# Keys of four attention layers kept in HBM by chunk and loaded 128 overlapping rows at a time

## Chip, cores and metric

One core of one Trainium2 chip. The metric is the device time of one execution in microseconds. A ratio is the mean time of one kernel's fast runs over that of the other's of the same rounds, so it is not quite the ratio of the medians quoted beside it.

## The reference

Four residual attention layers over 2048 positions of width 640, with 32 heads of 20 features. Layers 0 and 2 see a window of 256 keys, layers 1 and 3 see all keys.

```python
def layer(x, wqkv, wo, windowed):                 # condensed
    q, k, v = split_heads(layernorm(x) @ wqkv)    # 32 heads of 20
    scores = einsum("bhqd,bhkd->bhqk", q, k) * 20 ** -0.5
    scores = where(mask, scores, -1e9)            # layers 0 and 2 only: 0 <= i - j < 256
    return x + merge_heads(softmax(scores) @ v) @ wo
x = layer(x, A_wqkv, A_wo, True);  x = layer(x, B_wqkv, B_wo, False)
x = layer(x, A_wqkv, A_wo, True);  x = layer(x, B_wqkv, B_wo, False)
```

## The kernel before

Positions are cut into four chunks of 512, heads into eight groups of four. Each head of a group has a strip of 32 partitions, of which 20 hold features and 12 must add nothing to the product, so that PE multiplies four heads side by side. Projected blocks of 128 features cross the heads, so they go to HBM and come back in strips. Four loads fetch the queries and four the keys of a unit (a group and a chunk of queries). The buffers in SBUF were cleared once by VectorE, and the loads never touch the 12 rows.

```python
k_d = {l: dram.tile([D, S], ...) for l in range(4)}              # keys of a layer
...                                                              # t_block: a projected block is stored
dst = k_d[l][rows, c * C : (c + 1) * C] if n else q_d[l][c, rows, :]
nc.gpsimd.dma_start(out=dst, in_=staging.pop())
...                                                              # load_unit, layers 1 and 3
for j in range(4):
    rows = slice((4 * g + j) * DH, (4 * g + j + 1) * DH)
    strip = slice(32 * j, 32 * j + DH)
    nc.sync.dma_start(out=qt[key][strip, :], in_=q_d[l][c, rows, :])
    cols = slice(k0 * P, k1 * P)
    nc.sync.dma_start(out=kt[key][strip, cols], in_=k_d[l][rows, cols])
...                                                              # t_zeros, a task of the scheduler
yield ("wait", 12)
nc.vector.memset(ka_all[:, G + 1 : KA, :], 0.0)
yield ("wait", 3)
for n in range(2):
    nc.vector.memset(wop[:, 4 * n : 4 * n + 4, :], 0.0)
    yield ("wait", 3)
load_wop(0)                                                      # the output weights, 4 x 200 KB
...                                                              # then the memsets of kts and qts
for n in range(20):                                              # first_ln: unread, to raise PE's clock
    nc.tensor.matmul(ps[:, 0, :], lhsT=ident[:], rhs=ka_all[:, G, :], start=True, stop=True)
```

The whole program is emitted in the order that a scheduler in the kernel chooses, in steps (`wait` counts them). `wqk` are the weight tiles of the query and key projections, 160 KB each; they share SyncE's queue with the loads of keys and queries.

The softmax here doesn't subtract the row's maximum and nothing guards it: scores larger than these inputs give would overflow.

## Time and profile before

| | before |
|---|---|
| time, median of the three runs at hand | 2406.81 us (2402.35 to 2409.74) |
| ScalarE busy | 2194.2 us, 91% of the profiled 2411.7 us |
| PE's waits for weight tiles | 13.2 us in the first 500 us, 0.2 us after |
| PE's waits for keys | 1.8 us |
| loads of keys | 608, of 20 rows |

The page's engine line gives the bound, the waits give what a change of transfers could reach, and the timeline gives the order in SyncE's queue. These lines are shown in the prediction. In all profile lines PE is TensorE (PEld its weight loads), DVE is VectorE, ACT is ScalarE, POOL is GpSimd and SP is SyncE; SPq and POOLq stand for transfers that these two issue, and L354 is line 354 of that run's kernel. A row of the waits names who waited, for whom, the total in us, how often, and the longest.

### The profile page before, as it was taken

Reading aid. Unit: us, or ns where it says so; the run is one execution under the profiler, and the core shown is the slowest. Engines: PE = TensorE matmul, PEld = TensorE weight load, DVE = VectorE, ACT = ScalarE, POOL = GpSimd, SP = SyncE. Lnnn points to the kernel's source line nnn. Section 1 sums busy time; section 2 is a strip of 40 time slices with the busy share of each in tenths; the row PEclk is TensorE's granted clock in tenths of the full one; section 3 lists DMA queues with packets and bytes.
Section 4 is the critical chain, followed back from the end, with each engine's and each line's share of the span. In section 5 each row is a group of like instructions: output and inputs, shape, how many; then the busy total and the mean of one; then the engine's idle time right before and its main releaser. Section 6 shows DMA issues by size and latency. Waiting matters only on the chain.

```text
span 2411.7 us, 39997 instructions
## 1 busy us (share of the span) xinstructions
PE 2026.5 (84%) x15743; PEld 727.0 (30%) x15743; DVE 1278.8 (53%) x2485; ACT 2194.2 (91%) x1726; POOL 135.1 (6%) x284
## 2 busy tenths in 40 slices
PE   7888988888888898888888898888888788888886
PEld 3343333323323332333322333232322121122112
DVE  5776776423323344433352434452567767777776
ACT  6778789899999999999999989999999989999995
POOL 1111110000000001000100001001000000000000
PEclk9889999999999999999988989898755565556556
DMA  3323232322200233102330124112200010011000
GB/s 104 82 73 99 79 92 64 77 61 68 80 19 26 56 79 83 33 14 62 91 83 13 31 67 110 31 33 74 63 29 26 26 37 26 27 37 37 26 13 12
DMA packets 172796, 129.11 MB, mean 54 GB/s; under 512 B 115584, under 2 KB 155904, under 8 KB 172608
## 3 DMA queue, kind: packets, MB, share of 16 engines
q1 hardware_dynamic: 163872, 101.39, 16.9%
q0 software_dynamic: 8736, 25.18, 3.0%
q8 instruction: 123, 2.02, 0.4%
q14 instruction: 65, 0.53, 0.1%
HBM read 98.70 MB, written 27.79 MB: 52 GB/s over the span
## 4 chain that ended last, share of the span: by engine, by line
ACT 36%; PE 32%; issue 15%; DVE 12%; DMA 2%; SPq 1%; POOL 0%; ACTq 0%; DVEq 0%; POOLq 0%
ACT pt L1196 33%; PE ps L1176 8%; PE ps L350 6%; PE ps L1248 5%; PE ps L526 4%; PE ps L609 3%; PE ps L441 3%; ACT ka L1196 2%; DVE pt L1231 2%; DMA wqk<-in_B_wqkv_dram 1%; DVE on L992 1%; DVE st L301 1%; PE ps L405 1%; DVE oT L802 1%; DVE x_sb L535 1%
## 5 line engine op out<-in xcount | busy, mean ns | idle before, releaser
L1196 ACT ACTIVATE pt<-ps 128x1536 bf16<-128x1536 f32 (+3 forms) x1586 | 2053.3, 1443 | 160.8 <-PE ps L1176 148.7
L1176 PE MATMUL ps<-qt,kt 32*128 32x512 bf16 x4004 | 644.1, 464 | 224.9 <-ACT pt L1196 169.1
L1248 PE MATMUL ps<-pt,vt 128*21 128x512 bf16 x3744 | 466.7, 456 | 16.6 <-DVE oT L802 14.7
L1176 PEld LDWEIGHTS <-kt 32*128 32x128 bf16 x4004 | 188.2, 94 | 631.9 <-issue 612.2
L1231 DVE TENSOR_TENSOR pt<-pt,masks 128x1024 bf16<-128x1024 bf16 (+5 forms) x403 | 240.9, 625 | 167.5 <-ACT pt L1196 166.2
L350 PE MATMUL ps<-xnT,wqk 128*128 128x512 bf16 x830 | 223.3, 394 | 23.9 <-DMA wqk<-in_A_wqkv_dram 7.8
L609 PE MATMUL ps<-masks,ident 128*128 128x512 bf16 x749 | 231.4, 421 | 8.0 <-DVE st L301 2.5
L1248 PEld LDWEIGHTS <-vt 128*21 128x21 bf16 x4004 | 103.4, 90 | 351.8 <-issue 340.9
L301 DVE CAST st<-ps 128x512 bf16<-128x512 f32 x133 | 91.8, 690 | 199.7 <-PE ps L350 198.8
L526 PE MATMUL ps<-wop,on 128*128 128x320 bf16 x968 | 173.7, 321 | 8.3 <-DVE x_sb L535 4.4
L1176 PE MATMUL ps<-qa,ka 32*128 32x384 bf16 (+2 forms) x1408 | 118.6, 281 | 34.8 <-ACT pt L1196 31.0
L992 DVE TENSOR_TENSOR on<-oT,ps 128x512 bf16<-128x512 bf16 x128 | 87.5, 683 | 105.1 <-PE ps L988 102.1
L535 DVE TENSOR_TENSOR x_sb<-x_sb,ps 128x320 bf16<-128x320 bf16 x120 | 58.2, 485 | 149.5 <-PE ps L526 149.3
L840 DVE TENSOR_SCALAR xnT<-ps 128x512 int32<-128x512 f32 x92 | 63.5, 691 | 128.5 <-PE ps L834 125.3
L1196 ACT ACTIVATE ka<-ps 128x2048 bf16<-128x2048 f32 x65 | 127.4, 1960 | 2.7 <-PE ps L1176 2.2
L441 PE MATMUL ps<-wv,xnT 128*128 128x320 bf16 x640 | 113.2, 310 | 6.7 <-DVE on L992 1.4
L526 PEld LDWEIGHTS <-on 128*128 128x128 bf16 x968 | 90.2, 103 | 77.8 <-issue 41.8
L350 PEld LDWEIGHTS <-wqk 128*128 128x128 bf16 x830 | 71.0, 99 | 122.2 <-issue 48.6
L802 DVE CAST oT<-ps 128x512 bf16<-128x512 f32 x112 | 76.8, 685 | 49.3 <-PE ps L1248 35.8
L609 PEld LDWEIGHTS <-ident 128*128 128x128 bf16 x749 | 67.0, 103 | 115.9 <-issue 80.9
L1248 PE MATMUL ps<-pt,va 128*21 128x384 bf16 (+2 forms) x1408 | 80.1, 294 | 18.5 <-DVE oT L802 14.0
L981 DVE COPY rT<-ps 32x128 bf16<-32x128 bf16 x128 | 26.7, 209 | 93.1 <-PE ps L979 92.4
(91 smaller groups left out, 1434.7 us busy)
## 6 DMA issues: line engine op xcount, KB each, us to landing
vt<-v_d SPq DMA_DIRECT2D x48, 336.0 KB
kt<-k_d SPq DMA_DIRECT2D x192, 80.0 KB
wqk<-in_B_wqkv_dram SPq DMA_DIRECT2D x80, 160.0 KB
wqk<-in_A_wqkv_dram SPq DMA_DIRECT2D x70, 160.0 KB
k_d<-st POOLq DMA_DIRECT2D x75, 128.0 KB, 2.2
q_d<-st POOLq DMA_DIRECT2D x75, 128.0 KB, 2.2
qt<-q_d SPq DMA_DIRECT2D x384, 20.0 KB
v_d<-vs POOLq DMA_DIRECT2D x16, 336.0 KB, 3.6
```

Source lines behind the costliest of these rows:

```text
L301: nc.vector.tensor_copy(out=out_, in_=in_)
L350: nc.tensor.matmul(pq, lhsT=wt[:, dc, :], rhs=xt[:, dc, :], start=(dc == 0), stop=(dc == KD - 1),)
L441: nc.tensor.matmul(pv, lhsT=xt[:, dc, i * P : (i + 1) * P], rhs=wv_sb[l % 2][:, dc, h * HD : (h + 1) * HD], start=(dc == 0), stop=(dc == K ...
L526: nc.tensor.matmul(yp, lhsT=on[:, g, qb * P : (qb + 1) * P], rhs=wop[:, g, i * HD : (i + 1) * HD], start=(last or g == 0), stop=(g == G - 1),)
L535: nc.vector.tensor_tensor(out=xv, in0=had, in1=yp, op=ALU.add)
L609: nc.tensor.matmul(ps[:, b, :], lhsT=ident[:], rhs=masks[:, 0, :], start=True, stop=True)
L802: nc.vector.tensor_copy(out=oT[:], in_=op)
L992: nc.vector.tensor_tensor(out=on[:, g, :], in0=oT[:], in1=zb, op=ALU.mult)
L1176: nc.tensor.matmul(sp[:, i, col * P : (col + qn) * P], lhsT=u.k(kc, j), rhs=u.q(j, q0, qn), start=True, stop=True,)
L1196: nc.scalar.activation(out=pt[:, i:k, b0 * P :], in_=sp[:, i:k, b0 * P :], func=ACT.Exp, scale=SCALE,)
L1231: nc.vector.tensor_tensor(out=pt_[:, i:k, b0 * P :], in0=pt_[:, i:k, b0 * P :], in1=mv_, op=ALU.mult,)
L1248: nc.tensor.matmul(op[32 * j : 32 * j + VW, q0 * P : (q0 + qn) * P], lhsT=u.v(kc, j), rhs=pt[:, i, col * P : (col + qn) * P], start=(first ...
```

## The change

The intent is fewer and larger loads. Keys are stored by chunk. A load takes, for each of four heads, 32 consecutive rows, so 20 of the head and 12 of the next one, which meet zero rows of queries; 12 zero rows stand behind the last head. The key buffers then need no clearing. Separately, some of the unread matmuls move between the first transposes, and there are 22 of them in place of 20.

```diff
-    k_d = {l: dram.tile([D, S], BF16, ...) for l in range(4)}
+    k_d = {(l, c): dram.tile([D + 12, C], BF16, ...) for l in range(4) for c in range(NC)}
...
-        dst = k_d[l][rows, c * C : (c + 1) * C] if n else q_d[l][c, rows, :]
+        dst = k_d[l, c][rows, :] if n else q_d[l][c, rows, :]
...
+    def load_keys(l, g, c, dst):
+        src = k_d[l, c][4 * g * DH : (4 * g + 4) * DH, :].rearrange("(j e) s -> j e s", j=4)
+        src = bass.AP(tensor=src.tensor, offset=src.offset, ap=(src.ap[0], (C, 32), src.ap[2]))
+        nc.sync.dma_start(out=dst, in_=src)
...                                            # load_unit, layers 1 and 3
-            nc.sync.dma_start(out=kt[key][strip, cols], in_=k_d[l][rows, cols])
+        for cc in range(k0 // 4, k1 // 4):
+            load_keys(l, g, cc, kt[key][:, cc * C : (cc + 1) * C])
...                                            # t_zeros
-        nc.vector.memset(ka_all[:, G + 1 : KA, :], 0.0)
-        ready.add("kas")
-        yield ("wait", 3)
+        for n in range(4 * NC):
+            nc.gpsimd.dma_start(out=k_d[n // NC, n % NC][D : D + 12, :], in_=ka_all[0:12, G, :])
+            ready.add(("pad", n // NC))
+            yield ("wait", 1)
...                                            # the memsets of kts go, those of qts stay
-        for n in range(20):                    # first_ln: 14 first, then 3, 2 and 3 between transposes
+        warm(14)
...
+                warm((0, 3, 2)[i - 1])
...
+        warm(3)
```

## The prediction

> **What bounds the kernel now.** I read the page first, its engine line and its slices (40 slices of some 60 us, busy tenths).
>
> ```profile
> PE 2026.5 (84%) x15743; PEld 727.0 (30%) x15743; DVE 1278.8 (53%) x2485; ACT 2194.2 (91%) x1726; POOL 135.1 (6%) x284
> ...
> ACT  6778789899999999999999989999999989999995
> ...
> DMA  3323232322200233102330124112200010011000
> ```
>
> ScalarE, which does the exponentials, is busy 2194 of 2411.7 us. Its tenths are 9 almost everywhere, but 6 to 8 in the first eight slices. So the bound is ScalarE from about 480 us on, and before that nothing alone: the DMA queues carry little anywhere. The table by stage says the same (columns: busy us and instructions of PE, PE weight load, VectorE, ScalarE and GpSimd, then granted clock, DMA share, GB/s).
>
> ```profile
> 0.00:480.00 480.00, 416.08 (x3665) 175.19 (x3665) 320.29 (x734) 383.75 (x390) 66.96 (x149) 0.95 0.31 83
> 480.00:1740.00 1260.00, 1070.18 (x8714) 406.83 (x8710) 473.38 (x1043) 1188.54 (x898) 68.14 (x135) 0.93 0.22 56
> 1740.00:2412.00 672.00, 540.23 (x3374) 144.98 (x3371) 485.15 (x710) 621.95 (x439) 0.00 (x0) 0.54 0.10 28
> ```
>
> ScalarE idles 96 us in the first 480, 71 in the next 1260, 50 in the last 672. The change touches key loads, some VectorE memsets and the first 12 us. It removes no exponential, so it can only win inside these 217 us, mostly in the first 96. What PE waits for in the first 500 us (engine, line, releaser: us in total, times, longest) shows what is there for a change of loads:
>
> ```profile
> PE ps L1176 <- ACT pt L1196: 13.4, 25, 1.1
> PE ps L1248 <- DVE oT L802: 8.5, 7, 2.6
> PE ps L350 <- DMA wqk<-in_A_wqkv_dram: 7.8, 6, 2.6
> PE ps L405 <- DVE xn L396: 6.9, 8, 1.8
> PE ps L350 <- DMA wqk<-in_B_wqkv_dram: 5.4, 5, 1.7
> ```
>
> The waits are for weight tiles, 7.8 + 5.4 = 13.2 us. For keys, PE's waits in the whole run are 1.8 us (two, at 1410 us). **The key loads themselves are already hidden**; they matter by standing in SyncE's queue ahead of the weights.
>
> **What the Trainium skill says.** "DMA: Bandwidth & Descriptors", section "Why a DMA increments its semaphore by 16 and not by 1", says that a DMA from SyncE runs on k of the 16 DMA engines, the largest k up to 16 that divides the slowest dimension of both access patterns, on the lowest-numbered engines. For today's 20-row loads that gives k = 10. The trace agrees: each engine used leaves one 4-byte packet, and SyncE's queue has 16,928 of them. The 1216 loads of queries and keys by 10, the 40 of the output weights (20 rows) by 10, and the other 273 by 16 make 12,160 + 400 + 4,368 = 16,928, exactly. The new load has a source of 4 x 32 x 512 and a destination of 128 rows, so I expect **k = 4**.
>
> "Perfetto Trace Analysis", section "DMA Instruction — HWDGE (DVE, Sync)", says that the profiled time of an issue leaves out the movement of data. So I count 0.33 us of SyncE per issue (the trace's median for a key load is 327 to 328 ns, for the 128-row loads of values 344), and the movement apart, from the packets: median 46 ns for 1 KB, 159 ns for 4 KB, 18 ns for the 256 B packets of weights.
>
> "TensorE: Matmul & The Clock Gate", Part 1, says that PE's clock is halved after a window of some 3.4 us with too little activity. The trace's clock records agree: full from 6.32 us, half from 13.15 to 16.56 us (3.41 us), then full.
>
> "VectorE: DVE Perf Modes", section "Zero memsets can be issued as uint32 (trn2)", gives a cycle per 4-byte element. The trace shows the form, 128x2304 uint32, but in 1.98 us, 0.86 ns an element; I use that duration, not a cycle count.
>
> **The change, part by part.**
>
> *Start.* Today 20 unread matmuls run ahead of the first transposes.
>
> ```profile
> 2.75 6.24 PE L1032 MATMUL ps<-ka,ident 128*128 128x512 bf16 x20 [2.75 <-POOL ident L135]
> ...
> 8.82 0.72 PE L1050 MATMUL ps<-ident,xn 128*128 128x128 bf16 x10
> ...
> 12.37 3.70 PE L350 MATMUL ps<-xnT,wqk 128*128 128x512 bf16 x10 [0.78 <-ACT xnT L1073]
> ```
>
> The first normalised block is ready at some 7.46 us, while the last unread matmul starts at 8.60, so the transposes wait a microsecond. Then PE does little till 12.37, the clock is halved, and seven of the ten projection matmuls take 427 ns start to start, not 216: 7 x 0.21 = 1.5 us lost. With 14 ahead and 8 (3 + 2 + 3) between, the transposes start at about 7.65. That passes on only partly, since VectorE and GpSimd give the last block's scale at 9.52 us at the earliest: I take 0.4 us. If the clock holds, 1.5 us more. Sum **-1.9 us**.
>
> *Memsets.* Gone from VectorE are 1.98 us (key buffers, at 49.93 us) and 6 x 0.485 = 2.9 us (from 67 to 94 us), together 4.9 us. They stand in order before mask products and casts that PE waits for, and the first appears on the chain of waits with its full 1.98 us. I take three fifths: **-3.0 us**. In their place GpSimd issues 16 zero stores, at 0.54 us as its stores have today: 8.6 us on an engine busy 6%, from about 50 to 80 us. The delays are half a microsecond, and I count none. The output weights' load moves from 64.5 to some 92 us; its first user is at 110.5, so it stays hidden.
>
> *Fewer issues.* A windowed unit goes from 8 loads to 5, a unit of one key chunk from 9 to 6; a full unit of four chunks keeps 9. SyncE saves 3 x 0.37 = 1.1 us (an issue with its gap) ahead of a weight load in the first 480 us. The chain shows the case: weights wait at the end of such a row.
>
> ```profile
> 187.21 0.33 SPq L728 DMA_DIRECT2D qt<-q_d  x1
> 187.59 0.33 SPq L730 DMA_DIRECT2D kt<-k_d  x1
> 187.96 0.40 SPq L315 DMA_DIRECT2D wqk<-in_A_wqkv_dram  x1
> 188.40 0.59 SPq L315 DMA_DIRECT2D wqk<-in_B_wqkv_dram  x1
> ```
>
> Against it, one chunk on 4 engines is 32 packets of 1 KB per engine, 32 x 46 = 1.5 us, where four small loads took 8 packets, 0.4 us. So the weights start 1.1 us earlier behind a backlog of about 1.1 us more that partly drains meanwhile. I take a third of the 13.2 us: **-4.4 us**.
>
> *More bytes.* Key loads grow from 20 to 32 rows, 25.6 to 40.9 MB (estimate from the issue counts), some 15 MB on top of 101. For a full unit the four chunks queue on the same four engines: 4 x 1.5 = 5.9 us, against 8 packets of 4 KB, 1.3 us, today. A weight load just behind it uses all 16 engines and lands some 3.5 us later. Replaying SyncE's issue times with these packet costs (an estimate), 31 of the 84 weight loads after 480 us land over 2 us later. PE waits there for no weights at all today, so there is slack; I let a fifth or so of the 31 cost half a microsecond: **+3.5 us**, rounded up. The first loads of the last layer's first part (three chunks, 4.4 us on four engines) stand on the path at 1405 to 1412 us: **+2.0 us**.
>
> Sum: -1.9 - 3.0 - 4.4 + 3.5 + 2.0 = -3.8 us. From the median 2406.81 that is **2403 us**.
>
> **Rivals.** (a) *The four engines become a wait.* If most of the 31 late weight loads stall PE by 2 us, and windowed units by as much, the change costs 30 to 60 us and is slower, up to 2460. For it: k = 4 by the skill, and packets stretched to two or three times their median now and then (95th percentile of 1 KB packets 121 ns). Against it: keys are loaded one to two units (some 28 us each) ahead, PE and ScalarE have tiles in hand, and the mean load on those four engines stays moderate.
>
> (b) *SyncE's queue was the real brake of the first 480 us.* Then the relief frees more than the 13.2 us named, since a late weight tile holds later work too, up to 25 us: 2380. For it: weight loads stand repeatedly on the chain between 94 and 480 us. Against it: that stage has no single bound, so the next wait follows closely.
>
> (c) *All of it is hidden*, ScalarE being the bound for four fifths of the run: 2405 to 2407 and no more than the start gained.
>
> **Range and chances.** The three runs of before spread over 7 us, and my terms of either sign are 2 to 5 us, each uncertain by its own size; the two stage rivals reach further. So 2388 to 2416. 2% is 48 us: a gain of that size would need half of ScalarE's idle time of the first stage, a loss needs rival (a) in full. Faster 0.03, within 2% 0.95, slower 0.02.
>
> **What would show it.** In the profile after: some 1.9 us earlier first exponentials (17.19 us today) and ten projection matmuls in about 2.3 us; no key memsets; VectorE some 5 us less busy; 1 KB packets up by tens of thousands, and completion packets that fit k = 4; PE's wait for weights before 500 us down by some 4 us, and after 500 us a few microseconds where there were none; ScalarE's busy time unchanged. It is wrong if ScalarE's idle time between 480 and 1740 us moves by more than 10 us, or if the load runs on 16 engines.

## The result

The changed kernel takes 2435.39 us (median of four, 2429.07 to 2444.70), beside 2408.27 us (2402.35 to 2417.09). The ratio is 1.0113, with a 95% interval of 1.0066 to 1.016. It is within 2%, but slower, and **outside the predicted range** of 2388 to 2416.

The page of the changed kernel, its engine line and slices:

```profile
PE 2014.6 (82%) x15596; PEld 726.6 (30%) x15745; DVE 1274.4 (52%) x2478; ACT 2195.1 (90%) x1726; POOL 143.3 (6%) x300
...
ACT  6677789889989999999988989999899999999995
...
DMA  3333232222310134102231034213211111111100
```

Only GpSimd has more work, 143.3 us against 135.1, with its 16 zero stores. ScalarE is busy 2195.1 us against 2194.2, so nearly all of the 31 us between the two profiled runs is idle time of ScalarE. The stages of the changed kernel (columns as in the prediction) say when:

```profile
0.00:480.00 480.00, 404.38 (x3502) 170.09 (x3547) 309.14 (x714) 368.88 (x377) 71.68 (x160) 0.92 0.33 85
480.00:1740.00 1260.00, 1048.31 (x8521) 402.61 (x8623) 457.81 (x1017) 1173.05 (x889) 71.64 (x141) 0.93 0.24 63
```

In the first 480 us ScalarE did 368.9 us of work instead of 383.8, and in the next 1260 us 1173.1 instead of 1188.5. Both kernels run the same 1651 exponentials, so their starts can be compared one by one. The changed kernel is 1.85 us ahead at the first and 5.0 us ahead at the 51st (88 us into the run before). It is 8.8 us behind at the 101st (185 us), 14.6 at the 301st (459 us), 25.3 at the 351st (531 us) and 32.6 at the last. What PE waited for in its first 500 us, of transfers alone:

```profile
PE ps L354 <- DMA wqk<-in_A_wqkv_dram: 16.8, 4, 9.8
PE ps L354 <- DMA wqk<-in_B_wqkv_dram: 8.2, 3, 3.5
PE ps L1191 <- DMA ka<-k_d: 2.4, 1, 2.4
```

and after 500 us, where the kernel before waited less than 2 us for keys and 0.2 us for weights:

```profile
PE ps L354 <- DMA wqk<-in_B_wqkv_dram: 7.4, 3, 4.2
PE ps L842 <- DMA kt<-k_d: 2.8, 1, 2.8
PE ps L1191 <- DMA kt<-k_d: 2.5, 1, 2.5
PE ps L354 <- DMA wqk<-in_A_wqkv_dram: 2.3, 1, 2.3
PE ps L1191 <- DMA ka<-k_d: 1.5, 3, 1.1
```

Waits for weight tiles went from 13.2 to 34.7 us. Two rows of the timeline show the largest of them. SyncE's queue:

```profile
88.25 2.07 SPq L136 DMA_DIRECT2D wop<-in_A_wo_dram  x4
90.42 9.69 SPq L319 DMA_DIRECT2D wqk<-in_A_wqkv_dram  x4
```

and PE:

```profile
101.15 1.46 PE L354 MATMUL ps<-xnT,wqk 128*128 128x512 bf16 x3 [9.80 <-DMA wqk<-in_A_wqkv_dram]
```

The 800 KB of output weights, issued at 64.5 us before, now stand directly ahead of weight tiles that PE needs next. The first tile, issued at 90.42, lands 10.7 us later.

The other cause is a count. Each engine that a load uses leaves one 4-byte packet in SyncE's DMA queue: 12,096 of them now, 16,928 before. Without keys both kernels have 10,848, so the 312 key loads left 1248, exactly four each. **All keys now pass through 4 of the 16 DMA engines.** On the chain of waits, a weight tile issued just behind keys landed in the kernel before (start us, us, what) in

```profile
302.05 2.54 DMA wqk<-in_A_wqkv_dram
...
370.02 2.60 DMA wqk<-in_B_wqkv_dram
```

and in the changed kernel, right behind a single one-chunk load, in

```profile
489.00 5.06 DMA wqk<-in_B_wqkv_dram
...
500.83 4.57 DMA wqk<-in_B_wqkv_dram
...
512.73 4.38 DMA wqk<-in_B_wqkv_dram
```

These are not chosen cases. Counted from the completion updates in each trace, the weight tiles that SyncE issued directly after a load of keys (51 or 52 in every run) took from issue to landing, in the median, 2.70 us in the kernel before and 4.54 us in the changed one.

### The profile page after: what moved, and what is told of

It is laid out like the page before. It is cut to its first block, busy times and chain, and to the rows that moved or that the text cites.

```text
span 2443.0 us, 39483 instructions
## 1 busy us (share of the span) xinstructions
PE 2014.6 (82%) x15596; PEld 726.6 (30%) x15745; DVE 1274.4 (52%) x2478; ACT 2195.1 (90%) x1726; POOL 143.3 (6%) x300
## 4 chain that ended last, share of the span: by engine, by line
ACT 34%; PE 31%; issue 16%; DVE 12%; DMA 4%; SPq 1%; POOL 0%; ACTq 0%; DVEq 0%; POOLq 0%
ACT pt L1211 32%; PE ps L1191 8%; PE ps L354 6%; PE ps L1263 5%; PE ps L530 4%; PE ps L613 3%; PE ps L445 3%; ACT ka L1211 2%; DVE pt L1246 2%; DMA wqk<-in_A_wqkv_dram 1%; DVE st L305 1%; DMA wqk<-in_B_wqkv_dram 1%; DVE on L1000 1%; DVE oT L810 1%; PE ps L409 1%
## 5 line engine op out<-in xcount | busy, mean ns | idle before, releaser
L613 PE MATMUL ps<-masks,ident 128*128 128x512 bf16 x670 | 215.2, 416 | 14.5 <-issue 4.7
L1263 PE MATMUL ps<-pt,va 128*21 128x384 bf16 (+2 forms) x1408 | 80.4, 295 | 18.3 <-DVE oT L810 14.6
```

The costliest lines, as they stand in the source:

```text
L613: nc.tensor.matmul(ps[:, b, :], lhsT=ident[:], rhs=masks[:, 0, :], start=True, stop=True)
L1263: nc.tensor.matmul(op[32 * j : 32 * j + VW, q0 * P : (q0 + qn) * P], lhsT=u.v(kc, j), rhs=pt[:, i, col * P : (col + qn) * P], start=(first ...
```

## The experiments

Two causes were proposed: the moved load of the output weights, and the four engines. Rivals: the 15 MB more of traffic, the issue time in SyncE's queue, or the zero stores.

| run | edit | median us | beside it, before | ratio (95%) |
|---|---|---|---|---|
| e1 | the changed kernel again | 2440.69 | 2409.89 | 1.0123 (1.0086 to 1.0159) |
| e2 | output weights loaded early | 2434.32 | 2409.89 | 1.0092 (1.0055 to 1.013) |
| e3 | plain 128 rows, 16 engines (wrong result) | 2396.47 | 2409.89 | 0.9948 (0.9917 to 0.998) |
| e4 | e2 and e3 together (wrong result) | 2389.91 | 2409.89 | 0.9908 (0.9877 to 0.9939) |
| e5 | 32 rows a head in HBM, zeros by GpSimd | 2451.83 | 2408.06 | 1.0183 (1.0154 to 1.0213) |
| e6 | e2, keys in strips of 32 rows by chunk | 2426.32 | 2408.06 | 1.0073 (1.0052 to 1.0095) |
| e7 | two engines | 2501.39 | 2408.06 | 1.0389 (1.0366 to 1.0413) |
| e8 | before, unread matmuls moved | 2408.72 | 2408.06 | 1.0001 (0.9979 to 1.0024) |
| e9 | e5, zeros by SyncE at the start | 2393.20 | 2408.59 | 0.9926 (0.9897 to 0.9954) |
| e10 | before, output weights loaded late | 2415.60 | 2408.59 | 1.0025 (0.9995 to 1.0055) |
| e11 | e2, strips of 32 rows over all columns | 2406.45 | 2408.59 | 0.9989 (0.9953 to 1.0024) |

### e1: the changed kernel again

> The changed kernel unchanged, beside the kernel before on the same chip, as the yardstick for the three others of this call. Both theories: 1.011 times the kernel before (some 2435 us against 2408), PE waiting about 35 us for weight tiles (13 us before).

It took 1.0123 times the kernel before, and PE waited 33.9 us for weights. The loss repeats on this chip.

### e2: the output weights early

```diff
-        for n in range(4 * NC):
-            (zero store n; yield 1)
+        yield from pads(0, NC)                # the first layer's four zero stores
         (memsets of wop)
         load_wop(0)
+        yield from pads(NC, 4 * NC)           # the other twelve
```

> The changed kernel with only the order inside the start-up task altered: the load of the output weights (4 transfers of 200 KB) is issued after the first 4 of the 16 zero stores, so near 60 to 65 us as before, not at 88 us. Theory (the moved load stands ahead of the weight tiles in the DMA rings and holds PE for 9.8 us once, at 91 to 101 us): 9 to 11 us back, some 2425 us, ratio to before 1.007, PE's longest wait for a weight tile falls from 9.8 us to under 4. Rival (all of the loss is the key loads on four DMA engines; the weight tile would be late there anyway): 2433 to 2437, and a wait of several us for weights stays near 90 to 100 us.

The medians of e1 and e2 differ by 6.4 us, less than the 9 to 11 expected, and their intervals overlap. The time lies in the rival's range, and the longest wait did not fall under 4 us. The long wait is shorter but not gone: between 60 and 110 us PE waits once, for 5.6 us where e1 has 10.4. So four engines still make a weight tile late at the same spot. That the place of this load is a part of the loss, this run alone doesn't show; e4 and e10 add to it.

### e3: the same load on 16 engines, with a wrong result on purpose

```diff
-        src = (4 heads, 32 overlapping rows each)
-        nc.sync.dma_start(out=dst, in_=src)
+        b = (80 * g + 79) // P
+        nc.sync.dma_start(out=dst, in_=k_d[l, c][b * P : (b + 1) * P, :])
```

> Wrong result on purpose: each key load reads 128 contiguous rows of one projected block, so it has the same bytes, the same 1 KB packets and the same one issue, but a slowest dimension of 128 on both sides and so, if the rule holds, 16 DMA engines in place of 4 (16 completion packets a load: 312 x 16 = 4992 in place of 1248). The moved load of the output weights stays. Theory (four engines are what makes weights land late, beside the moved load): some 17 to 22 us back, 2413 to 2418 us, the waits for weights after 105 us near those of before, the 9.8 us wait at 91 us stays. Rival (more bytes and 1 KB packets in place of 4 KB are what costs, whatever the number of engines): stays within 5 us of the changed kernel, 2430 to 2437.

The relative error is 0.53, as intended. The time is 2396.47 us, 44 us less than e1, and 17 us less than the lowest that was expected. The completion packets are 15,840 = 10,848 + 312 x 16. Bytes, packets of 1 KB and the number of issues are those of the changed kernel, so the rival that blames traffic falls. The wait behind the output weights stays, at 6.4 us, and a tile directly after keys lands in 2.93 us (median). One doubt stayed: these loads read one projected block where the right ones sometimes need two, so they may wait less. e9 answers it.

### e4: both

> Both edits of the two runs above together (wrong result on purpose). Theory: the two losses are all there is and add up; what is left are the gains at the start (1.9 us) and of the missing memsets (3 us) and fewer issues, so 2398 to 2405 us, ratio to before 0.996 to 0.999. Rival (a third cost, such as the 15 MB more of traffic or the 16 zero stores): 2410 us or more.

2389.91 us, 6.6 us less than e3 and better than expected. By the medians, the place of the output weights is worth the same 6 to 7 us beside fast key loads (e3 to e4) as beside slow ones (e1 to e2); by the means it is 9.8 and 7.0. Between 60 and 110 us PE now waits 0.2 us for weights. Its waits for weights in the whole run are 6.5 us, where e2 has 29.8:

```profile
PE ps L354 <- DMA wqk<-in_A_wqkv_dram: 3.8, 3, 2.2
PE ps L354 <- DMA wqk<-in_B_wqkv_dram: 2.7, 2, 1.6
```

The pair that differs only in the key loads' engines (and in which rows they read), e2 and e4, is 44 us apart.

### e5: a correct kernel on 16 engines

Keys are kept with 32 rows a head, so four heads are 128 plain rows.

```diff
-        (l, c): dram.tile([D + 12, C], ...)
+        (l, c): dram.tile([32 * H, C], ...)
...
-        nc.sync.dma_start(out=dst, in_=src)                # load_keys
+        nc.sync.dma_start(out=dst, in_=k_d[l, c][P * g : P * (g + 1), :])
...                                                         # a block of 128 features is stored in 2 or 3 pieces:
+            (rest of a head, whole heads as (heads, 20, C), begin of a head)
...                                                         # pads: 384 KB a chunk from 12 partitions
+                out=k_d[l, c].rearrange("(h e) s -> e h s", e=32)[DH:32],
+                in_=ka_all[0:12, G, :].unsqueeze(1).to_broadcast((12, H, C)),
```

> Correct result. The changed kernel with the output weights loaded early, and keys kept in HBM with 32 rows a head (20 keys, 12 zero rows written once), so that a key load reads 128 plain rows: one issue, 16 DMA engines (4992 completion packets for 312 loads). The price: a projected block of 128 rows crosses heads and is stored in 2 or 3 pieces (13 stores a chunk in place of 5), and the zero rows are 384 KB a chunk. Theory (number of engines decides): as in the wrong-result run with both edits, 2385 to 2398 us, ratio 0.990 to 0.996. Rival (stores in pieces land later and GpSimd's queue becomes a wait): 2405 or more, with SyncE's waits for key stores growing by tens of us.

The rival's figure came, but not by its mechanism. The 100th exponential starts 50.5 us later than in the kernel before and the last one 39.7 us later: everything was lost in the first 185 us and some of it regained afterwards. Between 60 and 190 us PE waits for weights as follows:

```profile
PE ps L354 <- DMA wqk<-in_A_wqkv_dram: 51.0, 2, 32.1
```

and the list of issues (count, KB each, median us to landing) names what held the engines:

```profile
k_d<-ka POOLq DMA_DIRECT2D x16, 384.0 KB, 20.8
k_d<-st POOLq DMA_DIRECT2D x45, 120.0 KB, 3.3
```

A zero store of 384 KB, repeated from 12 partitions, took 20.8 us in the median (11.4 the first of a row, as the others queue behind it), while a 120 KB piece of a key store took 3.3. My own zeros spoilt this run, not the stores of keys.

### e6: 16 engines by four issues

```diff
-        nc.sync.dma_start(out=dst, in_=src)
+        for j in range(4):
+            r = (4 * g + j) * DH
+            nc.sync.dma_start(out=dst[32 * j : 32 * j + 32, :], in_=k_d[l, c][r : r + 32, :])
```

> Correct result. The changed kernel with the output weights loaded early, and each key load cut into four loads of 32 rows: the same bytes and packets, a slowest dimension of 32 and so 16 engines each, but four issues where there was one (1248 loads, 19968 completion packets). Theory (number of engines decides, issues matter little): 2390 to 2405 us, ratio 0.992 to 0.999. Rival (the count of issues in SyncE's queue decides): no better than the changed kernel with the early load of the output weights, 2425 to 2440.

2426.32 us, 8 us less than e2 (measured on another chip beside another set of runs: ratios 1.0073 and 1.0092), worse than expected and within the rival's range. The 30,816 completion packets fit 1248 loads on 16 engines. SyncE's issues of keys take 550 us in total here and 163.5 us in e2. A tile directly after keys lands in 2.73 us (median), as in the kernel before, and yet PE's waits for weights are still 30.6 us. e4, with the same bytes on 16 engines and a quarter of the issues, is 36 us faster. So issue time counts too, where it grows that much.

### e7: two engines

```diff
-        nc.sync.dma_start(out=dst, in_=src)
+        for h in range(2):
+            two = (heads 2 * h and 2 * h + 1 of src, 32 rows each)
+            nc.sync.dma_start(out=dst[64 * h : 64 * h + 64, :], in_=two)
```

> Correct result. The suspected cost doubled: each key load of the changed kernel is cut in two of 64 rows with a slowest dimension of 2, so all keys pass through 2 engines: 64 packets of 1 KB on each a chunk (64 x 46 ns = 2.9 us) in place of 32 on each of 4. Theory (the row of packets on the lowest engines delays what stands behind it): worse than the changed kernel by at least 30 us, 2465 to 2530 us, with PE's waits for weights at least twice the 34 us and new waits for keys. Rival (late weights in the changed kernel come from something else): within 10 us of the changed kernel, 2430 to 2450.

2501.39 us. PE's waits for transfers in the whole run:

```profile
PE ps L354 <- DMA wqk<-in_A_wqkv_dram: 42.1, 10, 12.6
PE ps L354 <- DMA wqk<-in_B_wqkv_dram: 29.6, 6, 11.2
PE ps L844 <- DMA kt<-k_d: 12.6, 1, 12.6
```

Twice the packets on half the engines doubled the waits for weights, 34.7 to 71.7 us, and a tile directly after keys lands in 5.24 us (median). e6 is the best comparison: SyncE spends 917 us issuing in both, the bytes and data packets are the same, and e7 is 75 us slower; some 5 to 10 us of that are the place of the output weights. GpSimd's key stores, which use the same engines, show the dose as well. The list of issues of before, and of e6 too, has

```profile
k_d<-st POOLq DMA_DIRECT2D x75, 128.0 KB, 2.2
```

of the changed kernel

```profile
k_d<-st POOLq DMA_DIRECT2D x75, 128.0 KB, 2.8
```

and of e7

```profile
k_d<-st POOLq DMA_DIRECT2D x75, 128.0 KB, 3.8
```

So 2.2, 2.8 and 3.8 us to landing, with keys loaded through 10 (e6: 16), 4 and 2 engines. The changed kernel stores keys to another layout than the kernel before, but e6 and e7 store them as it does. The stores of queries, which were not changed at all, follow less clearly: 2.2, 2.3 and 2.9 us.

### e8: the unread matmuls alone

> The kernel before with only the unread matmuls moved (14, then 3, 2 and 3 between the transposes). Both theories: 1.5 to 2 us earlier first exponential (15.3 to 15.7 us against 17.2), ten projection matmuls in 2.2 to 2.4 us, and the whole 0 to 4 us faster, ratio 0.998 to 1.000, so hardly clear of noise.

The edit is the last part of the change, on the kernel before. The first exponential starts 1.8 us earlier, but the whole is 1.0001 times the kernel before. 1.8 us is less than the interval is wide, so what is left of it at the end stays open. And a part of the 1.8 us differs from one execution to the next: e10, which starts exactly as the kernel before does, had its clock at full speed through all ten projection matmuls and its first exponential at 16.20 us, not 17.19.

### e9: the version that beats both

```diff
-                nc.gpsimd.dma_start(... 384 KB from 12 partitions ...)      # e5's zeros, in t_zeros
+        for n in range(1, 4 * NC):                                          # before the first task
+            for h in range(0, H, 8):
+                nc.sync.dma_start(
+                    out=k_d[n // NC, n % NC].rearrange("(h e) s -> h e s", e=32)[h : h + 8, DH:32, :],
+                    in_=ka_all[0:96, G, :],
+                )
```

> Correct result. The kernel with 32 rows a head in HBM, one plain load of 128 rows on 16 engines and the output weights loaded early, but with its zero rows (the burst that held a weight tile for 32 us in the earlier run of this layout) written by SyncE right after the first inputs, in pieces of 96 partitions, when PE needs no transfer. Theory (number of engines decides, the burst was what spoilt the layout): 2388 to 2400 us, ratio 0.992 to 0.997, PE's waits for weights under 15 us. Rival (key stores in 13 pieces a chunk delay what follows, or the 16 engines did not help in the wrong-result runs but the shorter dependencies did): 2408 or more.

The result is correct, in 2393.20 us, 0.9926 times the kernel before and clear of 1. It differs from e2 mainly in the engines of the key loads (16,320 completion packets: 10,848, 312 x 16 and 480 for the zeros) and is 41 us faster, as e4 was, but with the right dependencies. So the doubt of e3 is answered. Which change of the zero stores helped (their issuer, their time or their shape) was not separated. The waits of its whole run:

```profile
PE ps L354 <- DMA wqk<-in_A_wqkv_dram: 5.2, 3, 2.4
PE ps L354 <- DMA wqk<-in_B_wqkv_dram: 2.8, 4, 1.9
PE ps L1209 <- DMA kt<-k_d: 1.1, 1, 1.1
```

8.0 us for weights: under the 13.2 of the kernel before, which is what the prediction had hoped of the change.

### e10: the kernel before, output weights late

```diff
+        yield ("wait", 13)
         (memsets of wop)
         load_wop(0)
```

> Correct result. The kernel before with one thing changed: the task that clears and loads the output weights waits 13 scheduling steps more, as long as the zero stores hold it in the changed kernel. Theory (the place of this load costs by itself): 5 to 10 us slower than before, ratio 1.002 to 1.004, with one wait for a weight tile of 5 to 10 us near 90 to 105 us. Rival (it costs only together with the slow key loads): within 2 us, no such wait.

The load is issued at 90.5 us, and between 60 and 130 us PE waits for weights once:

```profile
PE ps L350 <- DMA wqk<-in_A_wqkv_dram: 7.8, 1, 7.8
```

The wait is there with the old key loads too, so the place costs by itself. The medians differ by 7.0 us; the ratio's interval just includes 1, so the size rests on three pairs whose medians agree (6.4, 6.6, 7.0 us), not on one.

### e11: more bytes, with the issues of before

```diff
-                k_d by chunk, one load of 4 x 32 rows a chunk
+                k_d by layer as before; out=kt[key][32 * j : 32 * j + 32, cols],
+                in_=k_d[l][rows.start : rows.start + 32, cols]
```

> Correct result. The changed kernel with the output weights loaded early, but keys laid out and loaded as before: four loads a unit over all its columns, only each of 32 rows in place of 20. So the 15 MB more are there, the memsets are gone, the issues are as many as before (608) and each load has 16 engines (9728 completion packets) in place of 10. Theory (engines and issue time decide, not bytes): 2398 to 2408 us, ratio 0.996 to 1.000. Rival (15 MB more of traffic costs by itself): 2415 to 2430.

2406.45 us, 0.9989 times the kernel before. The 15 MB more of keys, the zero stores and the missing memsets are all in it, and it is no slower. The completion packets, 20,576, fit 608 loads on 16 engines, so bytes are not quite alone here: each load has 16 engines in place of 10. But e3 and e4, with the bytes of the changed kernel, are faster than the kernel before. So bytes and zero stores are not the cause.

## Why the prediction was wrong

**Right.** ScalarE's work did not change. k = 4 was foreseen and counted. The first exponential came 1.85 us earlier (forecast 1.9), with PE's clock at full speed from 7.87 us for 34 us and the projection matmuls in 2.32 us (nine of the ten are in the trace). There was luck in it: against the start of e10 it is only 0.9 us, and the transposes began at 8.29 us, not at 7.65. Of the prediction's "seven" matmuls at 427 ns start to start the trace shows five, and one at 287; the stretch shrank by 1.38 us (3.70 to 2.32), near the 1.5 said. The memsets' gain was put at 3.0 us; the changed kernel gained 3.15 us from the 1st to the 51st exponential, but e8, which keeps the memsets, gained 1.4 us on the same stretch, so their share stays open.

**Failed: the output weights.** The step reads "The output weights' load moves from 64.5 to some 92 us; its first user is at 110.5, so it stays hidden." The place was right (88.25 us), but it was judged by its own user. The load is hidden, and it delays another: 800 KB lie in SyncE's queue ahead of weight tiles issued 2 us later. It cost some 7 us instead of 0 (6.4 to 7.0 by the medians of three pairs, 5 to 10 by the means).

**Failed: fewer issues.** The step reads "SyncE saves 3 x 0.37 = 1.1 us (an issue with its gap) ahead of a weight load" and "a backlog of about 1.1 us more that partly drains meanwhile. I take a third of the 13.2 us". An issue of the new kind takes 529 ns (median), not 327. All of SyncE's DMA issues sum to 584 us in the changed kernel and 567 us in the one before, so the whole run gained no issue time; in the first 480 us it fell, 187 to 158 us. And the backlog does not drain: the key load is issued last before the weights, so its 32 packets on each of four engines (mean 54 ns, 1.7 us) lie whole in front of them. In the median, tiles directly after keys now land 1.8 us later. The term was -4.4 us; in e2, with the output weights back in their place, PE's waits for weights before 500 us were still 20.4 us instead of 13.2.

**Undersized: full units.** "31 of the 84 weight loads after 480 us land over 2 us later", for +3.5 us, and +2.0 for the last layer's first loads. The mechanism was right. PE's waits for weights after 500 us were 9.7 us where there had been 0.2, and its waits for keys 6.8 us where the whole run had had 1.8. The prediction's own sign of being wrong came, too: ScalarE's idle time between 480 and 1740 us went from 71.5 to 87.0 us, by more than 10.

Rival (a), "The four engines become a wait", is what happened. It gave 30 to 60 us; the engines cost 41 to 44 us against 16 engines (e2 against e9 and e4), of which the kernel before, on 10 engines, may have had some already (not shown). The argument that the mean load of these engines is moderate was beside the point: a weight tile uses all 16 engines, so it has landed only when the fullest has done its part, 4.54 us in the median where it was 2.70. How the 27 us split between weights, keys and what each wait delays later is not settled to the microsecond, as profiled runs of one kernel differ by several.

## What to carry to other kernels

When several loads are merged into one, look at the slowest dimension of the merged access pattern before the count of issues: one load of 4 x 32 rows used four engines where four loads of 20 rows used ten each, and the weight tiles directly behind it landed 1.8 us later. A transfer that is early enough for its own user is not yet hidden: ask what is issued just after it. And check that a rare helper, such as zero fills, doesn't shift a large load into a crowded place by holding its task.

## What the Trainium skill lacked or had wrong

- "DMA: Bandwidth & Descriptors", on how many engines a DMA uses: right to the packet in every kernel that was counted (16,928, 12,096, 15,840, 30,816, 20,576 and 16,320 completion packets). It lacks what a small k costs those who queue behind: weight tiles directly behind keys landed 1.8 us later (median), and the kernel took 41 to 44 us more on 4 engines than on 16.
- The same page's rules for kernel authors say to coalesce many small transfers into one large one. Here 4 x 20 KB became 1 x 128 KB and the kernel slower. The proviso that k must not fall stands in another row of the same table, on using all 16 engines, which says that an outermost dimension under 16 confines a DMA to that many; the two rows don't refer to each other.
- The same page gives no issue time by shape: 327 to 328 ns for a load of 20 rows on 10 engines, 529 ns (median) for 4 x 32 rows on 4, 393 to 424 ns (medians of e9 and e3) for 128 plain rows on 16.
- No page gives the time of a store that repeats a few partitions: 384 KB from 12 partitions took 11.4 us to land from GpSimd when first of a row (20.8 in the median), where 120 KB of keys from 120 partitions took 3.3.
- "VectorE: DVE Perf Modes", zero memsets as uint32: the form is right, the time is not. The page counts one cycle per element and gives, in its opening table, a clock of 0.96 GHz, which would be 1.04 ns (worked out from the page); the trace's 1.98 us for 2304 elements and 0.485 us for 512 give 0.83 ns for each further element.
